# A branch prefetch hint for SyncE, beside the one for TensorE, at the end of a tuned kernel

## The chip, the cores and the metric

One Trainium2 chip, one core of it. Its engines run side by side, each through its own stream of instructions (before: TensorE is busy for 99% of the span, VectorE for 54%, GpSimd for 22%, ScalarE for 21%): TensorE (PE in the profile; PEld are its weight loads), VectorE (DVE), ScalarE (ACT), GpSimd (POOL) and SyncE (SP), which here mostly starts transfers (371 of its 614 records). A q behind a name (SPq) means the engine's instruction queue. The metric is the device time of the whole program in microseconds (us), the median of several executions. A profiled execution also gives a *span*, from the first to the last recorded instruction; it is some 1.7 us shorter than the time of the same execution (before: 1246.95 us of time, 1245.3 us of span).

## The reference, cut to what matters

Two independent layers whose outputs are joined: a state-space recurrence (A) and a segment-recurrent attention with memory (B).

```python
def reference(A_x, A_Lambda_re, ..., B_Wo, B_seg_len):
    # A: h = Lam_bar * h + Bu[t];  y = 2 Re(C h) + x * D      (2048 steps)
    # B: 64 segments of 32 tokens; each attends to itself and to 8 memory
    #    rows; the memory rows of a segment's output are the next one's memory
    ...
    return jnp.concatenate([a, b], axis=-1)
```

What matters here is how the kernel deals with B's chain of memories. It computes all segments at once from a guess of the memories, checks on the chip that the guess was good enough, and keeps a slow, exact loop behind a branch for when it was not. With the given inputs the check passes, so every engine *jumps over* the slow loop at the very end of the program. This jump is what the change is about.

## The kernel before

The last output blocks are written, then each engine loads the flag of the check and branches over the slow path. The numbers `L64`, `L1155`, `L1156` in the profile are these places (L64 is a helper through which SyncE's and TensorE's calls go; L1217 is the end of the program, which also carries the hints).

```python
    def out_last(self, ol):                    # the last 128 rows, in three pieces
        ...
            k.copy("vsv"[i], ot[:, c0:c1], p[:, 0:c1 - c0])
            k.SP.dma_start(self.out[0, T - 128:T, D + c0:D + c1], ot[:, c0:c1])
...
def hint(k):

    k.tc.mark_branch_hint_location("general", "LikelyTaken", engines=[mybir.EngineType.PE])
    i = k.nc.cur_bb.bb.instructions[-1]
    k.tc.keep_in_program_order(type("Ins", (), {"ins": i}))
...
        for n, (hp, u) in enumerate(at):       # attention; the experiments put a hint here
            if n == 12:
                k.SP.dma_start(wo0[:], b.Wo[:, :, 0:512])
...
                for n, _ in enumerate(b.outproj(tb, ol)):
                    if tb == 3 and n == 4:
                        hint(k)
...
        f0 = nc.values_load(b.flag[0:1, 0:1], min_val=0, max_val=1)                     # L1155
        with tc.If(f0 == 1, preferred_fallthrough_block=True, label="general"):         # L1156
            with tc.For_i(0, NSEG, 1) as it:
                with tc.tile_pool(name="gen", bufs=1) as gp:
                    b.general(it, gp)          # the slow path: not run here, but in the program
```

`hint` puts one instruction into an engine's stream that announces the branch named "general" as likely taken (in the trace of before a BRANCH_PREFETCH_HINT of 45 ns on TensorE). `preferred_fallthrough_block=True` asks for the slow path to be the code that follows the branch, so that the usual case is the taken branch, to code that lies behind the slow path.

Of the kernel before, what the change touches and what calls it, by code (L numbers as in the profile page):

```python
# [966 lines left out]

def hint(k):

    k.tc.mark_branch_hint_location("general", "LikelyTaken", engines=[mybir.EngineType.PE])  # L970
    i = k.nc.cur_bb.bb.instructions[-1]
    k.tc.keep_in_program_order(type("Ins", (), {"ins": i}))


def kernel_main(tc, A_x, A_Lre, A_Lim, A_Bre, A_Bim, A_Cre, A_Cim, A_logdt, A_Dskip, B_x, B_mem0, B_Wq, B_Wk, B_Wv, B_Wo, out,
                force=False, dbg=None):
    with ExitStack() as ctx:
# [157 lines left out]
        with pool("p4", "left") as p4:  # L1135
            b.p4 = p4
            ol = b.load_o_all(1)
            for _ in first:
                pass
            for tb in range(1, 4):  # L1140
                nx = b.load_o_all(tb + 1) if tb < 3 else None
                if tb == 3:
                    k.pin.add("PE")
                if tb == 1:
                    ck = b.check()
                    next(ck)
# [3 lines that stand above are left out]
                    if tb == 2:  # L1150
                        next(ck, None)
                ol = nx
# [69 lines left out]
```

## Time and profile before

| | before |
|---|---|
| time, median of 3 | 1246.7 us (1246.66 to 1246.81) |
| span of the profiled execution | 1245.3 us |
| TensorE matmul busy | 1234.2 us, 99% |
| end of the last arithmetic (a cast on VectorE) | 1239.74 us |
| SyncE: branch starts / next instruction starts | 1240.145 / 1243.003 us |
| last store: issued / last landing signal | 1239.77 / 1241.49 us |

The last two rows are from the individual records of the trace; the views below show them to a tenth.

The page (busy time by engine, then the shares of the chain of waits):

```profile
span 1245.3 us, 20124 instructions
...
PE 1234.2 (99%) x8270; PEld 662.5 (53%) x8342; DVE 667.7 (54%) x1250; ACT 263.4 (21%) x631; POOL 275.8 (22%) x407
...
PE 99%; issue 0%; DVE 0%
```

TensorE bounds the kernel almost to the end. But the chain ends with the last arithmetic instruction. What comes behind is not in it, because register, branch, semaphore and DMA-issuing instructions don't count as work. The timeline of the last stretch (start, duration, instruction, idle time before it) shows where that is:

```profile
1226.10 14.01 SPq L64 DMA_DIRECT2D out_dram<-b_ost  x4
...
1239.32 0.42 DVE L91 CAST b_ost<-psP 128x256 bf16<-128x256 f32 x1 [6.24 <-PE psP L64]
```

From 1239.74 us to the end of the span at 1245.3 us there are 5.5 us of tail. To read it, ask for the groups of the branch's line (count, shortest/median/longest duration in ns, first and last start):

```profile
L1156 SPq EVENT_SEMAPHORE  x8: 17/17/17, 1243.0 to 1243.5; - x8
...
L1156 ACTq COMPARE_BRANCH  x1: 58/58/58, 1236.4 to 1236.4; - x1
L1156 ACTq EVENT_SEMAPHORE  x1: 17/17/17, 1236.6 to 1236.6; - x1
L1156 PEldq COMPARE_BRANCH  x1: 418/418/418, 1237.8 to 1237.8; - x1
L1156 PEldq EVENT_SEMAPHORE  x1: 51/51/51, 1239.3 to 1239.3; - x1
L1156 DVEq COMPARE_BRANCH  x1: 72/72/72, 1240.0 to 1240.0; - x1
L1156 SPq COMPARE_BRANCH  x1: 58/58/58, 1240.1 to 1240.1; - x1
L1156 DVEq EVENT_SEMAPHORE  x1: 21/21/21, 1240.5 to 1240.5; - x1
```

Each engine has its branch (COMPARE_BRANCH) and then, at the target, its first semaphore instruction. The starts of the two are 0.2 us apart on ScalarE, 0.6 us on VectorE, and 2.86 us on SyncE, though SyncE's branch itself takes 58 ns. SyncE is the last engine to come to the end of the program: the first record of L1217 behind the branch starts at 1158.6 us on GpSimd, 1236.7 on ScalarE, 1239.5 on TensorE, 1240.6 on VectorE and 1243.6 us on SyncE. The waits of SyncE's queue over the last 30 us (who, for what: us in total, times, longest) have this stall too:

```profile
SPq L1156 <- SPq L1156: 2.8, 1, 2.8
```

SyncE "waiting for itself" is a sign that the view found no one else: the semaphore that this instruction asks for belongs to a store issued at 1170.8 us, whose last landing signal came at 1172.97 us. The wait is not for that store. The DMA view of 1240 to 1246 us (queue, kind: packets, MB, share) shows instructions being moved in this stretch:

```profile
q14 instruction: 3, 0.02, 1.2%
```

Three packets of 8 KiB, at 1241.34, 1241.37 and 1243.58 us. I take the queue to serve several engines: it moves 13 packets from 600 to 1238 us, of which a count of SyncE's instructions explains two. So much the trace shows: 2.86 us from SyncE's branch to its first instruction at the target, with two of the instruction packets moved in between. That SyncE waited for these packets is my reading; no record names what it waited for.

### The profile page before, as it was taken

The numbers are of one execution on the slowest core, as the hardware profiler recorded it, in microseconds if no ns is written. First come the engines' busy times: TensorE is split into PE (matmuls) and PEld (weight loads), VectorE is DVE, ScalarE is ACT, GpSimd is POOL, SyncE is SP. The second block draws the span as 40 slices with busy tenths as digits, with TensorE's granted clock in tenths as the row PEclk, the third lists the DMA queues.
The fourth block names the chain that finished last, engine by engine and source line by source line (L and its number), as shares of the span: only waits on it lengthen the run. The fifth ranks groups of instructions, "written<-read, shape, count | busy, mean of one in ns | idle before, by whom it ended". The sixth has DMA issues, their size and how long they took to land.

```text
span 1245.3 us, 20124 instructions
## 1 busy us (share of the span) xinstructions
PE 1234.2 (99%) x8270; PEld 662.5 (53%) x8342; DVE 667.7 (54%) x1250; ACT 263.4 (21%) x631; POOL 275.8 (22%) x407
## 2 busy tenths in 40 slices
PE   9999999999999999999999999999999999999998
PEld 5444444444455555556666656555665554446444
DVE  4688899998711124666666666666666641001000
ACT  5344444443310000211112111111211110000000
POOL 4111331212332321322222222222222220000000
PEclk9999999999999999999999999999999999999999
DMA  9965444554898734664454545545553379407000
GB/s 248 272 191 147 131 135 127 144 155 107 242 322 248 249 116 95 196 170 124 96 145 108 144 108 120 132 92 121 120 142 92 65 211 230 107 18 153 17 26 19
DMA packets 316246, 176.83 MB, mean 142 GB/s; under 512 B 138874, under 2 KB 301550, under 8 KB 316150
## 3 DMA queue, kind: packets, MB, share of 16 engines
q1 hardware_dynamic: 294054, 147.95, 47.8%
q10 hardware_dynamic: 21072, 24.38, 5.9%
q0 software_dynamic: 1024, 3.17, 0.7%
q8 instruction: 66, 1.08, 0.4%
q14 instruction: 30, 0.25, 0.1%
HBM read 89.14 MB, written 53.17 MB: 114 GB/s over the span
## 4 chain that ended last, share of the span: by engine, by line
PE 99%; issue 0%; DVE 0%
PE psP L64 82%; PE psU L64 9%; PE psS L64 3%; PE psO L64 2%; PE psR L64 2%; DVE b_xe L91 0%; DVE b_ost L91 0%; DVE a_n L962 0%; DVE hpb L105 0%; DVE ones L102 0%
## 5 line engine op out<-in xcount | busy, mean ns | idle before, releaser
L64 PE MATMUL psP<-b_xe,b_wq 128*128 128x480 bf16 (+1 forms) x1280 | 247.7, 343 | 0.1
L64 PE MATMUL psP<-b_xe,b_wk 128*128 128x480 bf16 (+1 forms) x1280 | 247.7, 343 | 0.0
L64 PE MATMUL psP<-b_wv,b_xe 128*128 128x512 bf16 (+2 forms) x1033 | 223.4, 372 | 0.8
L644 POOL TENSOR_TENSOR b_m<-b_e,maskB 99x396 bf16<-99x396 bf16 x160 | 139.8, 874 | 338.5 <-ACT b_e L641 338.5
L641 ACT ACTIVATE b_e<-psS 99x396 bf16<-99x396 f32 x176 | 88.2, 501 | 536.7 <-PE psS L64 533.4
L64 PEld LDWEIGHTS <-b_wk 128*128 128x128 bf16 x1280 | 119.4, 98 | 94.2
L64 PEld LDWEIGHTS <-b_wq 128*128 128x128 bf16 x1280 | 118.7, 98 | 87.7
L64 PEld LDWEIGHTS <-b_xe 128*128 128x128 bf16 x1056 | 101.8, 98 | 119.1 <-DVE b_xe L91 0.2
L91 DVE CAST b_k<-psP 128x480 bf16<-128x480 f32 (+1 forms) x192 | 97.4, 528 | 100.9 <-PE psP L64 100.9
L91 DVE CAST b_q<-psP 128x480 bf16<-128x480 f32 (+1 forms) x192 | 97.4, 528 | 93.1 <-PE psP L64 91.5
L64 PEld LDWEIGHTS <-b_ol 128*128 128x128 bf16 x864 | 84.3, 98 | 94.4
L64 PE MATMUL psU<-a_xT,a_bt 128*128 128x512 bf16 x493 | 113.9, 379 | 1.1
L64 PE MATMUL psP<-t,a_hl 128*128 128x512 bf16 x496 | 112.1, 379 | 0.8
L91 DVE CAST b_ost<-psP 128x512 bf16<-128x512 f32 (+1 forms) x17 | 11.5, 676 | 177.4 <-PE psP L64 176.3
L64 PE MATMUL psP<-wo,b_ol 128*128 128x512 bf16 (+1 forms) x440 | 91.9, 364 | 0.4
L64 PE MATMUL psP<-t,b_ol 128*128 128x512 bf16 x408 | 91.7, 379 | 0.4
L280 POOL TENSOR_SCALAR a_tt<-a_pr,a_tabf 128x1 f32<-128x1 f32 x48 | 34.1, 710 | 243.2 <-DVE a_pr L275 243.2
L661 DVE TENSOR_TENSOR b_ob<-psO,b_accR 99x384 bf16<-99x384 f32 x160 | 85.9, 553 | 2.4 <-DVE b_accR L660 0.4
L89 ACT ACTIVATE b_vst<-psP 128x512 bf16<-128x512 f32 x126 | 71.9, 589 | 71.3 <-PE psP L64 59.9
L267 DVE TENSOR_TENSOR a_pr<-psU,a_tabf 128x2048 f32<-128x2048 f32 x32 | 73.0, 2282 | 15.7 <-PE psU L64 14.0
L64 PEld LDWEIGHTS <-a_bt 128*128 128x128 bf16 x512 | 49.2, 98 | 57.6
L64 PEld LDWEIGHTS <-a_hl 128*128 128x128 bf16 x512 | 49.0, 98 | 56.7
(200 smaller groups left out, 962.7 us busy)
## 6 DMA issues: line engine op xcount, KB each, us to landing
b_v<-b_vx SPq DMA_DIRECT2D x16, 1122.0 KB
b_wv<-in_B_Wv_dram SPq DMA_DIRECT2D x16, 1024.0 KB
b_vx<-b_vst ACTq DMA_DIRECT2D x24, 544.0 KB
b_on<-b_ob SPq DMA_DIRECT2D x15, 720.0 KB
a_hs<-a_h SPq DMA_DIRECT2D x32, 256.0 KB
b_wog<-in_B_Wo_dram SPq DMA_DIRECT2D x4, 2048.0 KB
b_wq<-in_B_Wq_dram SPq DMA_DIRECT2D x16, 512.0 KB
b_wk<-in_B_Wk_dram SPq DMA_DIRECT2D x16, 512.0 KB
```

Source lines behind the costliest of these rows:

```text
L64: r = f(*a, **kw)
L89: self.S.activation(out, in_, ACT.Copy)
L91: self.V.tensor_copy(out, in_)
L267: V.tensor_tensor(pr[:], u[:].unsqueeze(1).to_broadcast([128, 2, 2, TB]), view(t3, [[TB + 1, 2], [TB + 1, 2], [1, TB]]), ALU.mult)
L280: G.tensor_scalar(tt[:, j:j + 1], w[:, j, TB - 1:TB], t3[:, 1, TB:TB + 1], None, ALU.mult)
L641: k.S.activation(e[:], s[0:GW, :, :, 0:GW], ACT.Exp, scale=float(E) ** -0.5, accum_out=self.accE[0:GW, i:i + 1])
L644: k.G.tensor_tensor(m[0:GW, 0:4 * GP].rearrange("p (a b q) -> p a b q", a=2, b=2)[:, :, :, 0:GW], e[:], mask[0:GW, :, :].unsqueeze(2).to_b ...
L661: V.tensor_tensor(self.ob[:, b0:b0 + n, :], o[0:GW, 0:n, 0:E], r.unsqueeze(2).to_broadcast([GW, n, E]), ALU.mult)
```

## The change

TensorE already had a hint ahead of its branch. The change gives SyncE one at the same place of the program, to get rid of that stall.

```diff
 def hint(k):
 
-    k.tc.mark_branch_hint_location("general", "LikelyTaken", engines=[mybir.EngineType.PE])
-    i = k.nc.cur_bb.bb.instructions[-1]
-    k.tc.keep_in_program_order(type("Ins", (), {"ins": i}))
+    for e in (mybir.EngineType.PE, mybir.EngineType.SP):
+        k.tc.mark_branch_hint_location("general", "LikelyTaken", engines=[e])
+        i = k.nc.cur_bb.bb.instructions[-1]
+        k.tc.keep_in_program_order(type("Ins", (), {"ins": i}))
```

## The prediction

Its sum is complete: 2.0 us gained if the hint works, 1244.7 us. One sentence, on the cause of the stall, is cut where marked, because no run shows what it said. The 0.5 us after which SyncE resumes is my estimate, given without its source.

> **What bounds the kernel.** The busy table has TensorE matmul busy for 1234.2 of 1245.3 us (99%), and the chain of waits is TensorE for 99%, at a full granted clock. The change touches no matmul. It can only act on the tail: the chain ends with the last cast (1239.32 us, 0.42 us long), and the span ends at 1245.3 us. So about 5.5 us of tail lie behind the arithmetic.
>
> **The tail before (groups of the lines of the branch and of the kernel's end, and the records of the SyncE queue).** SyncE issues the last store at 1239.77 us (0.33 us long); its last landing signal comes at 1241.49 us. SyncE's compare-and-branch starts at 1240.145 us and takes 58 ns; its next instruction starts only at 1243.00 us. That is a stall of 2.80 us, with instruction packets on queue 14 at 1241.34, 1241.37 and 1243.58 us. The same branch costs GpSimd and ScalarE 0.13 us and VectorE 0.51 us. After it, eight semaphore waits about 0.075 us apart (the eighth needs the last store), then 1.7 us of further waits and barriers. All other engines have been waiting since 1240.7 us or earlier. So SyncE's branch is on the critical path. [...]
>
> **What the change is worth if the hint works.** SyncE resumes 0.5 us after the branch, near 1240.7 us; seven waits run to 1241.25; the eighth waits for the landing, 1241.49, so it ends near 1241.55 instead of 1243.56. Gain: about 2.0 us, not 2.8, because the store's landing becomes the limit. Time near 1244.7 us.
>
> **Why I doubt that it works.** The hint goes into SyncE's stream at the fifth output group of the last block, some ten SyncE instructions ahead of the branch. TensorE's hint ran at 1214.45 us, and in the DMA view no packet at all moves in 1214 to 1219 us; the next instruction packet of its queue comes at 1225.6 us, right on the regular cadence of 27.6 us. So a hint seems to fetch nothing itself: it redirects the next regular fetch. TensorE has one between its hint and its branch. SyncE's own fetches (I assign queue 14's at 122.0, 381.6, 641.6 and 896.9 us to it by counting its instructions; they lie about 128 apart) put the next regular one some three instructions behind the branch, so none falls between hint and branch. One added instruction moves this by one place, not enough. Then the hint costs one issue of some 45 ns (TensorE's hint: 45 ns) in a queue that is waiting anyway, and nothing is won.
>
> I give 60% to no effect (1246.7), 40% to the 2.0 us gain. Both are far within 2%; nothing here can give or take 25 us.
>
> **What would show it.** No effect: SyncE again has about 2.8 us between its branch and its next instruction, and queue 14 has its packets after the branch. Effect: that gap falls to about 0.5 us, a queue-14 packet appears between 1212 us and the branch, SyncE's last wait of the eight ends just behind the landing, and the span ends near 1243.3 us. In both: matmul busy, the chain and everything up to 1239.7 us unchanged; the hint itself near 1212.6 us, right behind a store.
>
> **What would make it wrong.** The hint may fetch at once where the queue has room; the shift by one instruction may move a regular fetch ahead of the branch; the scheduler may place the hint elsewhere or reorder stores around it; or an engine that I see waiting may turn out late.

## The result, and the profile after

| | before | after |
|---|---|---|
| time, median | 1246.76 us (1246.66 to 1247.15, 4 runs) | 1247.03 us (1246.64 to 1248.60, 4 runs) |
| span of the profiled execution | 1245.3 us | 1244.9 us |
| SyncE: branch starts / next instruction starts | 1240.145 / 1243.003 us | 1239.822 / 1242.681 us |
| last store: issued / last landing signal | 1239.77 / 1241.49 us | 1239.45 / 1241.04 us |

The ratio of after to before is 1.0004, with a 95% interval of 0.9987 to 1.0021: no difference. (Ratios here are the record's, over the fast runs of the same rounds, so not quite the ratio of the medians quoted.)

The page and the groups of the branch's line after (its lines have moved down by one, L1156 is now L1157):

```profile
span 1244.9 us, 20197 instructions
...
PE 1237.5 (99%) x8342; PEld 662.1 (53%) x8342; DVE 668.1 (54%) x1250; ACT 263.1 (21%) x631; POOL 275.9 (22%) x407
```

```profile
L1157 SPq EVENT_SEMAPHORE  x8: 17/17/17, 1242.7 to 1243.2; - x8
...
L1157 PEldq COMPARE_BRANCH  x1: 413/413/413, 1237.5 to 1237.5; - x1
...
L1157 SPq COMPARE_BRANCH  x1: 78/78/78, 1239.8 to 1239.8; - x1
```

(The instruction count is up by 73, but 72 of those are matmuls that the trace of before had missed: 8270 records against 8342 weight loads. One instruction is new, the hint.) SyncE's queue waits and the instruction packets of 1240 to 1246 us:

```profile
SPq L1157 <- SPq L1157: 2.8, 1, 2.8
```

```profile
q14 instruction: 3, 0.02, 1.3%
```

The stall is there, 2.86 us again, with its three packets. And the hint did run, where it should (the groups of the program's end):

```profile
L1218 SPq BRANCH_PREFETCH_HINT  x1: 60/60/60, 1212.3 to 1212.3; - x1
L1218 PEldq BRANCH_PREFETCH_HINT  x1: 45/45/45, 1214.1 to 1214.1; - x1
```

It ran 27 us ahead of the branch and changed nothing. The span is 0.3 us shorter because everything of this execution, from the last matmul on, came 0.3 us earlier; the tail behind the last cast is as long as before (5.52 us; before, 5.51 us).

### The profile page after: what moved, and what is told of

It is laid out like the page before. It is cut to its first block, busy times and chain, and to the rows that moved or that the text cites. A ratio compares the mean times of both kernels' runs of the same rounds, so it can differ in the third digit from the quotient of the medians.

```text
span 1244.9 us, 20197 instructions
## 1 busy us (share of the span) xinstructions
PE 1237.5 (99%) x8342; PEld 662.1 (53%) x8342; DVE 668.1 (54%) x1250; ACT 263.1 (21%) x631; POOL 275.9 (22%) x407
## 4 chain that ended last, share of the span: by engine, by line
PE 99%; DMA 0%; DVE 0%; SPq 0%; issue 0%
PE psP L64 83%; PE psU L64 9%; PE psS L64 3%; PE psO L64 2%; PE psR L64 2%; DMA b_xr<-in_B_x_dram 0%; DVE b_ost L91 0%; SPq L64 0%
```

## The experiments

The question is why a hint that ran 27 us early did not help, and what would. Theory A, as the prediction had it: SyncE's instructions come by regular fetches, and a hint only steers such a fetch. The trace of before has these packets, which I assign to SyncE by counting: 121.96, 381.65, 641.56 and 896.89 us, 8192 bytes each, 130, 126 and 128 of SyncE's recorded instructions apart. *Page*, in the expectations too, is my word for what one packet brings. The packet near 897 us is the last of these before the branch, which is the 124th recorded instruction behind it (the 125th in after). At 128 apart, an estimate from these counts, the next fetch would come three or four instructions *behind* the branch, and the hint stands nine instructions ahead of it. So, by the theory, no fetch is left to steer. Rivals are named in the expectations.

The gaps below are from SyncE's branch to its next instruction, start to start, in the profiled execution. Executions differ by a few tenths of a us in their absolute times, so compare gaps, and the *tail*: from the end of the last cast to the end of the span, in the same execution.

| run | what | SyncE's gap, us | later stall | tail, us | time, us (runs) | before in the same rounds |
|---|---|---|---|---|---|---|
| before | TensorE's hint only | 2.86 | none | 5.51 | 1246.76 (4) | |
| after | SyncE's hint at 1212 us | 2.86 | none | 5.52 | 1247.03 (4) | 1246.76 (4) |
| b_fill8 | before + 8 idle instructions on SyncE | 0.53 | none | 3.32 | 1244.87 (5) | 1246.76 (9) |
| a_fill8 | after + the same 8 | 0.54 | none | 3.32 | 1244.49 (5) | 1246.76 (9) |
| a_early | SyncE's hint at 738 us | 0.54 | none | 3.34 | 1244.80 (1) | 1246.76 (9) |
| b_nopehint | before without any hint | 0.52 | 1.49 us | 4.81 | 1246.71 (1) | 1246.76 (9) |
| c_ahead | SyncE's hint at 873 us | 0.54 | none | 3.40 | 1244.91 (5) | 1247.05 (9) |
| c_behind | SyncE's hint at 904 us | 2.99 | none | 5.65 | 1246.96 (4) | 1247.05 (9) |
| b_fill2 | before + 2 idle instructions on SyncE | 2.67 | none | 5.31 | 1246.81 (1) | 1247.05 (9) |
| b_poolhint | the hint on GpSimd only | 2.91 | none | 5.57 | 1247.38 (1) | 1247.05 (9) |
| d_actstore | after, last store from ScalarE's queue | 2.67 | none | 3.35 | 1245.13 (5) | 1246.89 (9) |
| a_again | after, unaltered | 2.97 | none | 5.63 | 1247.04 (4) | 1246.89 (9) |

All gave correct results. Runs with several executions had them all in the fast state; of a single execution the state is unknown, and only its gaps and its tail are used. No time differs from before by 2%; where a ratio's 95% interval leaves 1 out, the text gives it.

### Move the branch instead of the hint: b_fill8, a_fill8, b_fill2

```diff
+def fill_sp(k, n):
+
+    for _ in range(n):
+        k.tc.keep_in_program_order(k.nc.sync.drain())
...
                     if tb == 3 and n == 4:
                         hint(k)
+                        fill_sp(k, 8)        # 2 in b_fill2
```

The drains land in SyncE's stream at 1212 us, where SyncE has nothing to do for 13.5 us (before: stores issued at 1212.28 and 1226.10 us). They are there to take up places; the SyncE drains in the trace of before take 7 to 13 ns each. One clause of a_fill8's expectation is cut where marked: the distance from the branch to its target, which no run shows.

> The kernel before, no SyncE hint, with 8 drains that do nothing put into SyncE's stream behind the store at 1212 us, where SyncE waits anyway. They push the branch 8 places on, so that SyncE's regular fetch (in the kernel before about 3 instructions behind the branch) falls some 5 ahead of it, near 1233 us. Theory A (position: the branch stalls because the next regular fetch had not been made yet, and a hint only steers that fetch): a queue-14 packet near 1234 us, SyncE's gap after the branch falls from 2.80 to 0.1-0.5 us, the span by about 2.0 us, time near 1244.7 us. Rival B (SyncE pays 2.8 us for any taken branch out of its page, fetched or not, and only a working hint saves it): gap stays 2.8 us, time 1246.7 us.

> The changed kernel (SyncE hint) with the same 8 drains behind the hint, so that one regular fetch lies between hint and branch. Theory A: like the run with drains alone, gap 0.1-0.5 us, time near 1244.7 us; the hint adds nothing[...]. Rival B: the hint works once a fetch lies between, gap under 0.6 us here and 2.8 us with the drains alone. Rival C (the hint is without effect on SyncE and the position too): 2.8 us in both.

> The kernel before with 2 idle drains in place of 8: the branch moves 2 places, the next regular fetch (3 to 4 places behind it) still comes after it. Theory A: gap 2.86 us, 1246.7 us. If any extra work in SyncE's stream at 1212 us helps (the drains as such, rival E): 0.53 us, 1244.8 us.

Measured, b_fill8, branch and target on SyncE:

```profile
L1163 SPq EVENT_SEMAPHORE  x8: 17/17/17, 1240.9 to 1241.6; - x8
...
L1163 SPq COMPARE_BRANCH  x1: 58/58/58, 1240.4 to 1240.4; - x1
```

The gap is 0.53 us. The time fell to 1244.87 us, a ratio of 0.9985 (0.9971 to 0.9998), *without any hint on SyncE*. The DMA view of 600 to 1238 us counts queue 14's packets ahead of the branch; first the kernel before, then b_fill8:

```profile
q14 instruction: 13, 0.11, 0.1%
```

```profile
q14 instruction: 14, 0.11, 0.1%
```

One more fetch ahead of the branch, at 1227.80 us (I had expected it near 1234 us, one or two SyncE instructions later). Two drains were not enough: 2.67 us, with the packets behind the branch. So eight places matter and two don't. In these runs the gap goes with the side of the branch on which the packet falls (0.53 us with it ahead, 2.67 us with it behind), not with there being extra work. The hint together with the drains (a_fill8) has the same gap as the drains alone, 0.54 us and the same ratio, 0.9985. Rivals B, C and E are out. (That the packet at 1227.80 us held the target is not shown.) In the profiles the tail fell by 2.20 us, from 5.51 to 3.32, not by the 2.33 us by which the gap shrank: the eighth of the waits at the target now starts 0.21 us behind the seventh in place of 0.07, and it is the one that asks for the last store's semaphore (landing in before: 1241.49 us), as the prediction's sum had it. The medians differ by 1.9 us; the rest is scatter of whole executions.

### Move the hint: a_early, c_ahead, c_behind

```diff
-def hint(k):
+def hint(k, engines=(mybir.EngineType.PE,)):
 
-    for e in (mybir.EngineType.PE, mybir.EngineType.SP):
+    for e in engines:
...
         for n, (hp, u) in enumerate(at):
+            if hp == 11 and u == 6:          # c_ahead; a_early: 8, 0; c_behind: 12, 4
+                hint(k, (mybir.EngineType.SP,))
```

> The changed kernel with SyncE's hint moved up, 204 instructions ahead of the branch, so that one regular fetch of SyncE (897 us) lies between hint and branch. If a hint turns the next regular fetch, whichever it is, to the target (as my prediction had it): the fetch near 897 us brings the target, SyncE's gap at the end falls to about 0.5 us, time near 1244.7 us, perhaps with a stall of some 2.8 us of SyncE somewhere between 900 and 1100 us that nobody waits for. If it steers only the fetch made inside the page of the branch, which comes too late here: gap 2.8 us, time 1246.7 us.

> The changed kernel with SyncE's hint some 8 SyncE instructions ahead of SyncE's last regular fetch (the packet near 897 us), at about 873 us. Theory A (the hint steers one fetch, the one made when SyncE enters the page that holds the branch; it must have run by then): gap after the branch about 0.54 us as with the hint at 738 us, no packet between 897 us and the branch for SyncE, time near 1244.8 us. Rival D (a hint needs many microseconds or many instructions to act): 2.86 us, 1246.7 us.

> The same with the hint 13 instructions on, some 4 instructions behind that fetch (about 904 us), still 121 instructions and over 330 us ahead of the branch. Theory A: the fetch is already made, gap 2.86 us, time near 1246.8 us. Rival D (time ahead is what counts, 27 us in the change were too few): 0.54 us and 1244.8 us.

Measured: the hint ran at 737.8, 872.8 and 904.1 us, and SyncE's regular fetch came near 896.7 us in all three. The hints of c_ahead, then of c_behind:

```profile
L1220 SPq BRANCH_PREFETCH_HINT  x1: 60/60/60, 872.8 to 872.8; - x1
```

```profile
L1220 SPq BRANCH_PREFETCH_HINT  x1: 60/60/60, 904.1 to 904.1; - x1
```

The branch's groups of c_ahead, then of c_behind:

```profile
L1159 SPq EVENT_SEMAPHORE  x8: 17/17/17, 1240.6 to 1241.4; - x8
...
L1159 SPq COMPARE_BRANCH  x1: 78/78/78, 1240.1 to 1240.1; - x1
```

```profile
L1159 SPq EVENT_SEMAPHORE  x8: 17/17/17, 1242.9 to 1243.5; - x8
...
L1159 SPq COMPARE_BRANCH  x1: 78/78/78, 1239.9 to 1239.9; - x1
```

Thirteen SyncE instructions apart, the two placements differ by the whole effect: 0.54 and 2.99 us; 1244.91 us (ratio to before 0.9983, 0.9970 to 0.9997) and 1246.96 us (1.0000, 0.9985 to 1.0015). Both hints ran more than 300 us ahead of the branch, so rival D, lead time, is out. The packets of queue 14 show how the early hint works. Counted in 600 to 1238 us and in 1240 to 1246 us, c_ahead has

```profile
q14 instruction: 13, 0.11, 0.1%
```

```profile
q14 instruction: 2, 0.02, 0.7%
```

c_behind, with the hint too late, has 13 in the first window too, and in the second

```profile
q14 instruction: 3, 0.02, 2.0%
```

Before: 13 and 3. So the hint adds no fetch, and one less comes behind the branch. That it makes the fetch near 897 us bring the target in place of something else is my reading; no trace shows what a packet holds. SyncE had no new stall of that size in between, so the hint cost nothing here.

One thing these runs can't tell: whether the hint must come ahead of *any* next fetch or of the last one before the branch. In all of them these are the same fetch. (The second theory of a_early took the one in the branch's page for a later fetch; as it stands there, it is out, at 0.54 us.)

### Does a hint do anything on TensorE, and what does it do to SyncE: b_nopehint, b_poolhint

```diff
-                    if tb == 3 and n == 4:
-                        hint(k)
```

```diff
-    k.tc.mark_branch_hint_location("general", "LikelyTaken", engines=[mybir.EngineType.PE])
+    k.tc.mark_branch_hint_location("general", "LikelyTaken", engines=[mybir.EngineType.Pool])
```

> The kernel before without its TensorE hint, to see whether a hint does anything on this chip. If TensorE's hint works: without it TensorE stalls some 2.8 us after its branch (1238.2 to about 1241 us, before: at most 1.1 us, and it waited for a semaphore then), an instruction packet of queue 8 starts between 1238.9 and 1240 us and a second one behind it; time unchanged at 1246.7 us, because SyncE ends later. If it does not: TensorE's records at the end stay as they are, one packet after the branch.

> The kernel before with its one hint on GpSimd in place of TensorE. Without any hint SyncE had a gap of 0.52 us after the branch and a stall of 1.49 us eleven waits on; with TensorE's hint it has 2.86 us and no later stall, though its own instructions are the same. Theory L (any hint to this branch, on whatever engine, changes where the program puts the branch's target, for SyncE out of the fetched page): SyncE's gap 2.86 us again and no later stall. Theory R (SyncE's two pictures are chance, or TensorE's own doing): 0.52 us and 1.49 us. TensorE, now without its hint, stalls some 3.9 us in either; the time may stay near 1246.7 us.

The first diff is b_nopehint, the second b_poolhint. Their groups of the branch's line, TensorE and SyncE, in this order:

```profile
L1154 SPq EVENT_SEMAPHORE  x8: 17/17/17, 1241.1 to 1241.8; - x8
...
L1154 PEldq COMPARE_BRANCH  x1: 3861/3861/3861, 1238.2 to 1238.2; - x1
...
L1154 SPq COMPARE_BRANCH  x1: 58/58/58, 1240.6 to 1240.6; - x1
```

```profile
L1156 SPq EVENT_SEMAPHORE  x8: 17/17/17, 1243.4 to 1244.0; - x8
...
L1156 PEldq COMPARE_BRANCH  x1: 3841/3841/3841, 1238.1 to 1238.1; - x1
...
L1156 SPq COMPARE_BRANCH  x1: 58/58/58, 1240.5 to 1240.5; - x1
```

TensorE's hint works in these runs: its branch takes 3861 or 3841 ns without it (I had expected some 2.8 us) and 418 ns with it. (On TensorE the stall shows as the branch's own duration, on SyncE as a gap behind it.) Here too it saves a fetch behind the branch: from 1238 us on, TensorE's queue 8 moves one packet in before and two in b_nopehint. It wins no time here, because SyncE ended later (b_nopehint: TensorE's next instruction at 1242.1 us, SyncE's stalled wait at 1243.53 us).

The surprise is SyncE in b_nopehint. I had expected nothing to change there, and its gap is 0.52 us, with no hint of its own. In exchange it stalls 1.49 us eleven instructions further on, between two of its closing waits (starts at 1242.04 and 1243.53 us), so most of what the gap won is lost again. Not all: the tail of b_nopehint is 4.81 us, 0.7 us shorter than that of before. Its one execution took 1246.71 us with a last cast 0.46 us later than in the profile of before, so whether the kernel without any hint is faster is not shown. With the hint on GpSimd instead, which has nothing to do with SyncE, the gap is 2.91 us again and the later stall is gone. Theory L's gaps came, for the two engines tried and in one execution each: with a hint to this branch, on TensorE or on GpSimd, SyncE stalls at the target (2.86 and 2.91 us) and not later; without one, it has 0.52 us at the target and 1.49 us later.

Why it does so is not shown. That a hint moves the target to another place in the program, as theory L has it, was my guess: no run shows the addresses of the branch, of its target or of what the packets bring.

### Does the stall cost time only because SyncE is last: d_actstore, a_again

```diff
-            k.SP.dma_start(self.out[0, T - 128:T, D + c0:D + c1], ot[:, c0:c1])
+            (k.nc.scalar if i == 2 else k.SP).dma_start(self.out[0, T - 128:T, D + c0:D + c1], ot[:, c0:c1])
```

> The changed kernel with its very last store (64 KB) issued from ScalarE's queue, so that SyncE reaches its branch 3.5 us earlier, near 1236.4 us. Theory A (SyncE's stall costs time only because it is the last thing between the last store and the barrier): the stall is still there, 2.86 us, but over by 1239.3 us, ahead of the landing at about 1241.4 us; the span falls by about 2.0 us, time near 1244.9 us, the same as with the hint in its right place. Rival F (the end is held by something else that the hint in its right place also changed): 1246.9 us.

> The changed kernel once more, unaltered, to compare with the other run on one chip and to see whether its time differs from before at all. Theory A: gap 2.86 us and the time of before within its spread (about 1246.3 to 1248 us); the earlier median 0.3 us above before was chance. If the hint costs something: again 0.3 us or more above before.

Measured, d_actstore (SyncE's branch, then its eight waits at the target):

```profile
L1157 SPq EVENT_SEMAPHORE  x8: 17/17/17, 1239.5 to 1241.5; - x8
...
L1157 SPq COMPARE_BRANCH  x1: 78/78/78, 1236.8 to 1236.8; - x1
```

The stall is still 2.67 us, but SyncE comes to it 3.5 us earlier against the last cast (3.08 us ahead of the cast's end; 0.40 us behind it in after), because it has no last store to issue. It is over at 1239.5 us; the eighth wait then ends with the landing, at 1241.5 us. Time 1245.13 us, ratio 0.9987 (0.9973 to 1.0001, so just not clear of 1), tail 3.35 us (c_ahead 3.40). The instruction packets come apart here: 1237.80 us, inside SyncE's stall; 1240.07 us, 0.6 us after it; and 1241.46 us, 1.3 us behind VectorE's branch (1.4 us in before). So the stall is harmless where it is not last, and what is left of the tail, the landing and about 1.7 us of waits and barriers behind it, is common to all good versions.

The change itself, run again: gap 2.97 us, 1247.04 us, ratio 1.0001 (0.9986 to 1.0017). The 0.3 us by which its first median lay above before is within the scatter: nine executions of before in one set of rounds lay between 1246.52 and 1248.19 us.

c_ahead beats before by about 2 us (0.17%), and by as much c_behind, in the same rounds, whose hint comes too late like that of the change. It does so with the hint that the change meant to add. b_fill8, a_fill8 and d_actstore do as well within the scatter.

## Why the prediction was right or wrong

The sentences in quotation marks are the prediction's, in part shortened.

- **"TensorE bounds the kernel; the change can only act on the tail": right.** The busy share is 99% in both traces, and nothing ahead of the last cast changed but by the scatter.
- **"SyncE's branch is on the critical path, 2.80 us": right.** Every version that took the stall away without a new one, or took it from the end of the chain, has a tail of 3.32 to 3.40 us in place of 5.51. (b_nopehint put 1.49 us in its place and has 4.81 us.)
- **"About 2.0 us, not 2.8, because the store's landing becomes the limit": right.** b_fill8 1.9 us, c_ahead 2.1 us between the medians, and in both the eighth wait came 0.21 and 0.28 us behind the seventh (0.07 us in before), just after the landing. The 0.5 us to resume, from which this sum starts, came without a reason given; 0.52 to 0.54 us were measured.
- **"The hint redirects the next regular fetch, and none falls between hint and branch": right in what it foretold.** With no SyncE fetch between hint and branch the change did nothing (2.86 us); whether the fetch was redirected, no packet shows. b_fill2 and b_fill8 bracket the fetch at two to eight places behind the branch (three were predicted; the packet at 1227.80 us in b_fill8, seven instructions ahead of its branch, speaks for the low end); c_ahead and c_behind show that here the hint had to come before the packet at 896.7 us (hint at 872.8 us: 0.54 us; at 904.1 us: 2.99 us).
- **"One added instruction moves this by one place, not enough": right** (even two are not enough).
- **The number: wrong.** The step that failed is the last one, "60% to no effect (1246.7), 40% to the 2.0 us gain". The doubt was right and led to no gain; the term that was mis-sized is the gain, by its 40% share: weighted as stated, that is 0.8 us and a time of 1245.9 us. The runs showed a gain of 0 in its place: a gap of 2.86 and 2.97 us, a tail of 5.52 and 5.63 us (before 2.86 and 5.51), ratios 1.0004 and 1.0001 in two sets of rounds. Of what the prediction names as possible errors, "the hint may fetch at once where the queue has room" would have given that gain; after the hint at 1212.3 us queue 14 moved nothing before 1240.79 us, behind the branch. I had the evidence for it, the 1214 to 1219 us without a packet behind TensorE's hint, and did not trust it. A second fault lies in "no effect (1246.7)": that is the median of three executions within 0.15 us. After's own four spread over 2.0 us (1246.64 to 1248.60), and their median lies 0.3 us above it with a tail as long as before.
- **Not seen: why SyncE stalls at the target at all.** I took it as given. In b_nopehint and b_poolhint, one execution each, the stall goes with a hint on another engine: 0.52 us without any (and 1.49 us later), 2.91 us with GpSimd's; before, with TensorE's, has 2.86 us.
- **"If it works, a queue-14 packet appears between 1212 us and the branch": wrong for a working hint.** It appears with the drains (1227.8 us); a hint in its right place adds no packet, and one less comes behind the branch (c_ahead 13 and 2, before 13 and 3).

## What to carry to other kernels

In this kernel a hint was not a fetch (no packet at all in 1214 to 1219 us behind TensorE's at 1214.45 us): look for the instruction packets of the engine's queue, find the last one ahead of the branch, and put the hint in front of it (ahead of SyncE's packet at 896.7 us it left a gap of 0.54 us, behind it 2.99 us), for each engine by its own count of instructions, since the same place in the source is a different distance in each stream (in after nine instructions ahead of the branch on SyncE; 134 weight loads, besides the matmuls, lie between on TensorE). Where the stall came, it was 2.67 to 2.99 us on SyncE (gap) and 3.84 to 3.86 us on TensorE (the branch's own duration). When a program's tail matters, look behind the end of the chain of waits, at the branch and semaphore instructions that don't count as work, and ask which engine reaches the barrier last; taking the last store off that engine's queue did as much as the hint (tails of 3.35 and 3.40 us). And when two outcomes are possible, predict the likelier one and let the range hold the other.
